# Spaced weight pieces, a later second block and split evictions in a fused attention, feed-forward and top-1 expert kernel

## The chip, the cores and the metric

One core of a Trainium2 chip runs the whole kernel. The metric is the device time of one launch in microseconds (us); lower is better. The profile comes from one execution of the same program.

## The reference, cut to what matters

Three layers follow each other: causal attention with a forget gate, a dense feed-forward layer, and a mixture of eight experts of which each token uses one. The change touches the middle layer alone.

```python
def _moe_ref(x, w_in, w_out):            # x: 2304 x 512, w_in: 512 x 2048, w_out: 2048 x 512
    h = x @ w_in
    g = np.where(h >= 1, h, np.where(h <= -1, 0.0, (h + 1) ** 2 / 4))
    return (g @ w_out).astype(np.float32)

x = attention(q, k, v, f)                # 4 x 8 heads x 576 tokens x 64, brought to 2304 x 512
x = _moe_ref(x, w_in, w_out)             # the weights are float64
return _moe2_ref(x, ...)                 # gate, 8 experts of 512 x 1024 x 512, top 1
```

## The kernel before, in words

**Precision.** Each product is made of three matmuls: operands are split into a high and a low part (`h`, `l`), and high x high, low x high and high x low are summed. So an activation block needs a cast and a subtraction (ACT and DVE for a loaded block, ACT and POOL for hidden values), and so does a weight.

**Halves.** The hidden width of 2048 is done in two halves of 1024, each with its own layer object: `half0` (tiles `hp`, `accp`, weights `wa`) starts while attention still runs; `half1` (tiles `hr`, `accr`, `accBr`, weights `wb`) follows and adds the stored result of half0. Then comes the expert layer (`hm`, `accm`). A half works through token blocks. Half0 has five blocks of 256 tokens and then two of 512 (n = 5 and 6); half1 has four of 512 and one of 256. A block has eight units, one for each 128 hidden columns: a first product (`first`, 12 matmuls into one hidden bank `hp` or `hr`), a middle on the vector engines (`ffn_hidden`: ACT `tp`, DVE `gp` twice, ACT `ghp`, POOL `glp`), and a second product (`ffn_second`, 12 matmuls into four accumulators of one PSUM bank each for a wide block). There are two hidden banks, two pairs of `gh`, `gl`, one `t`, one `g`, and one set of accumulators.

**Weights.** `float64_weights` loads a half's weights in 16 pieces of 512 KB (a0, b0, a1, b1, ... a7, b7: `a` serves a unit's first product, `b` its second). A piece is a DMA on SP's queue (L819) and a serial chain on one working buffer `wx`: ACT L828, DVE L829, L831, L833, L835, ACT L839, POOL L840. Two raw buffers (`wr_b`) and one working buffer (`wx_b`) are all there is.

**The order.** All instructions are put in order by a planner when the program is built: generators ask for engines and buffers, and the planner takes its own prices and its own clock (`o.now`, in ns) to decide which operation is next on which engine. On the chip only the order of each engine's queue and the waits on data are left: a time in the planner holds nothing back on the chip, it only places an operation behind others. Every queue, SP's too, runs in order. The planner's price for a wide unit's two products is

```python
def mm(n, k=1):
    return k * max(111.0, n * 0.458)      # 2 x mm(512, 12) = 5628 ns
```

**Around the change.** `late_pools` runs when attention's last result is stored; it makes half1's weights object and starts its 16 pieces with the due times `[0.0] * 2 * NF`, so that a piece starts as soon as a raw buffer is free. When half0's last first product is planned (`half0.first_done`), `half1.loads` asks for its blocks 0 and 1, for which there are buffers; `load_wide` issues four DMAs for a block and then four pairs of ACT L870 and DVE L871. `ffn_finish0` empties the accumulators of a wide block of half0, one after another: ACT L1051 (`x_0a`), DVE L1048 (`x_0b`), ACT (`x_1a`), DVE (`x_1b`). The next block's second products wait for this.

Of the kernel before, what the change touches and what calls it, by code (L numbers as in the profile page):

```python
# [14 lines left out]
ALU = mybir.AluOpType  # L15
# [3 lines left out]
P = 128  # L19
# [5 lines left out]
def f32(ap):  # L25
    return ap.bitcast(F32)
# [12 lines left out]
NP_ = 8  # L39
NSUM = 4  # L40
FIRST_WEIGHTS = [6000.0 + 2700.0 * n for n in range(5)] + [20500.0 + 5200.0 * n for n in range(11)]
WARM_FROM, WARM = 1500.0, 0.6


# [31 lines left out]
class Order:  # L76
# [90 lines left out]
    def done(self, ev):  # L167
        ev.n -= 1
        if ev.n == 0:
            for g in ev.waiters:  # L170
                self.at(self.now, lambda g=g: self.step(g, None))
            ev.waiters = []

    def give(self, res, ids):
        res.ids += ids
        while res.waiters:
            gen, n = res.waiters[0]
            got = res.take(n)
            if got is None:
                return  # L180
            res.waiters.pop(0)
            self.at(self.now, lambda gen=gen, got=got: self.step(gen, got))
# [8 lines left out]
def dve(n, fn, prio=5.0, fast=False):  # L191
    return Use("DVE", 144 + n * (0.6 if fast else 1.05), fn, prio)


def act(n, fn, prio=5.0, more=0.0):
    return Use("ACT", 155 + n / 1.2 + more, fn, prio)
# [10 lines left out]
def dma(nbytes, fn, prio=5.0, eng="SP", k=1):  # L207

    hold = 550.0 if eng == "SP" else 1000.0

    def after(o):
        o.dma_free = max(o.dma_free, o.now + hold + 650.0) + nbytes / 245.0
        return max(o.dma_free, o.now + hold * k + 650.0 + nbytes / k / 245.0) + 1000.0
    return Use(eng, hold * k, fn, prio, after)
# [9 lines left out]
def kernel(  # L224
# [14 lines left out]
    nc = tc.nc  # L239
# [6 lines left out]
    KC = DM // P  # L246
    TB = 256
# [3 lines left out]
    FH = w_in.shape[1] // 2  # L251
    NF = FH // P
# [11 lines left out]
    o = Order()  # L264
    go, give, done = o.spawn, o.give, o.done
# [509 lines left out]
    def wide_x(ids, name):  # L775

        gp = late["gp"]
        if ids[0] == 2:
            t = gp.tile([P, 2, KC, 2 * TB], F32R, tag="xA", name=name, bufs=1)
            return [[t[:, hl, c] for c in range(KC)] for hl in range(2)]  # L780
        t = gp.tile([P, 2, 2, 2 * TB], F32R, tag="xB", name=name, bufs=1)
        f = [fp.tile([P, 2, 2 * TB], F32R, tag=f"x{n}0", name=name + n, bufs=1) for n in "hl"]
        return [[f[hl][:, 0], f[hl][:, 1], t[:, hl, 0], t[:, hl, 1]] for hl in range(2)]
# [16 lines left out]
    def float64_weights(W, src_a, src_b, times, prio):  # L800

        a = src_a.rearrange("(c p) f -> p c f", p=P)
        b = src_b.rearrange("(c p) d -> p c d", p=P)
        ah, al, bh, bl = W.t
        n = 0
        for fc in range(NF):
            cs = slice(P * fc, P * fc + P)
            for src, hi, lo, ok in ((a[:, :, cs], ah[:, :, cs], al[:, :, cs], W.ok[0][fc]),
                                    (b[:, fc:fc + 1], bh[:, fc:fc + 1], bl[:, fc:fc + 1],
                                     W.ok[1][fc])):  # L810
                yield times[n]
                g = yield (wr_b, 1)
                go(float64_piece(g, src, hi, lo, ok, W.name, prio))
                n += 1
# [44 lines left out]
    def load_wide(src, w, ok, name, ev):  # L859
        yield ok  # L860
        g = yield (xl_b, ((2,), (0, 1)))

        def put():
            hi, lo = wide_x(g, name)
            for c in range(KC):
                nc.sync.dma_start(f32(lo[c])[:, :w], src[c])
            return hi, lo
        hi, lo = yield dma(P * KC * w * 4, put, 1, k=4)
        for c in range(KC):
            yield act(w, lambda: nc.scalar.copy(hi[c][:, :w], f32(lo[c])[:, :w]), 1)  # L870
            yield dve(w, lambda: nc.vector.tensor_tensor(  # L871
                lo[c][:, :w], f32(lo[c])[:, :w], f32(hi[c])[:, :w], ALU.subtract), 1)
        ev.x = ([x[:, :w] for x in hi], [x[:, :w] for x in lo], g)
        done(ev)
# [46 lines left out]
    class Layer:  # L921
# [15 lines left out]
        def loads(self):  # L937
            for n in self.blocks:
                if self is half0 and n < NARROW:
                    if n == 0:  # L940
                        continue
                    yield self.src_ok[n]
                    go(load_block(self.src[n], self.src_ok[n], f"{self.name}x{n}", self.x_ok[n]))
                else:
                    yield self.src_ok[n]
                    go(load_wide(self.src[n], self.widths[n], self.src_ok[n], f"{self.name}x{n}",
                                 self.x_ok[n]))

# [59 lines left out]
    def ffn_second(acc, fc, W, gh, gl):  # L1008
        bh, bl = W.t[2:]
        narrow = acc[0].shape[1] == TB  # L1010
        w = gh.shape[1]
        for ip, (b, g) in enumerate(((bh, gh), (bl, gh), (bh, gl))):
            for d in range(KC):
                nc.tensor.matmul(acc[d][:, :w], b[:, fc, P * d:P * d + P], g,  # L1014
                                 start=(fc == 0 and ip == 0 and (not narrow or d % 2 == 0)),
                                 stop=(fc == NF - 1 and ip == 2), skip_group_check=True)

    def moe_second(acc, fc, W, gh, gl):
        bh, bl = W.t[2:]
# [13 lines left out]
    def keep(dst, r, ok, g):  # L1033
        def put():
            for i in range(2):
                nc.sync.dma_start(dst[2 * i:2 * i + 2].rearrange("c p t -> p c t"), r[i])
        yield dma(P * KC * TB * 4, put, 2, k=2)
        done(ok)
        if g is not None:
            give(x2_b, g)  # L1040

    def ffn_finish0(n, acc):
        if n >= NARROW:
            g = yield (x2_b, ((0, 1),))
            r = wide_r(f"x2_0_{n}")
            for d in range(KC):
                if d % 2:
                    yield dve(2 * TB, lambda: nc.vector.tensor_scalar(r[d], acc[d], 4.0, None,  # L1048
                                                                      ALU.mult), 0)
                else:  # L1050
                    yield act(2 * TB, lambda: nc.scalar.mul(r[d], acc[d], 4.0), 0)  # L1051
            go(keep_first(n, r, g))
            return
        g = yield (x2_b, 1)
        r = [x.rearrange("p (d t) -> p d t", d=2) for x in x2_half(g[0], f"x2_0_{n}")]
        acc = late["acc0"]
        yield act(2 * TB, lambda: nc.scalar.mul(r[0], acc[:, 0:2], 4.0), 0)
        yield dve(2 * TB, lambda: nc.vector.tensor_scalar(r[1], acc[:, 2:4], 4.0, None,
                                                          ALU.mult), 0)
        go(keep(x2p[n], r, x2p_ok[n], g))  # L1060

    def keep_first(n, r, g):
        t0, w = FIRST[n]
# [53 lines left out]
    def late_pools():  # L1117

        yield att_ok
        psa.release()  # L1120
        ap.release()
        late["wp2"] = tc.alloc_tile_pool(name="wp2", bufs=1, side="right")
        late["gp"] = gp = ctx.enter_context(tc.tile_pool(name="gp", bufs=1))
        late["psg"] = ctx.enter_context(tc.tile_pool(name="psg", bufs=1, space=PSUM))
        late["nat_b"] = Buffers(2)
        late["gt_b"], late["gl_b"] = Buffers(1), Buffers(1)
        give(h_b, [1])
        give(xl_b, [1, 2])
        give(x2_b, [1])
        W = late["W1"] = Weights(late["wp2"], "wb")  # L1130
        go(float64_weights(W, w_in[:, FH:], w_out[FH:], [0.0] * 2 * NF, 4))
        for n, shape, dt in (
            ("es", [E, 2], F32),
            ("ie", [P, KC, P + E], F32), ("itau", [P, 1], F32), ("iota", [P, E], F32),
            ("tid", [P, NTT], I32), ("ones", [P, P], F32), ("upper", [P, P], F32),
            ("sidx", [P, NSLOT], F32), ("tinit", [P, NROW // P, 2], F32), ("ss", [P, 2, NTT], F32),
            ("lg", [P, NTT, E], F32), ("oh", [P, NTT, E], F32), ("gate", [P, NTT], F32),
            ("gj", [P, DM], F32), ("fold", [P, Q], F32), ("gm", [P, NTT - TL], F32),
        ):
            G[n] = gp.tile(shape, dt, name=n)  # L1140
        go(gate_setup())
        go(prev_loads())
        done(late_ok)
# [476 lines left out]
    def static_slots():  # L1620
# [11 lines left out]
        for ok in late_w["M"].ok[0] + late_w["M"].ok[1]:  # L1632
# [8 lines left out]
    half1 = Layer("r", wide, lambda: late["W1"], xw, [att_ok] * NW, ffn_hidden, ffn_second,  # L1641
                  ffn_finish1, 6)
# [23 lines left out]
    with tc.manual_schedule():  # L1666
        go(attention())
        go(float64_weights(W0, w_in[:, :FH], w_out[:FH], FIRST_WEIGHTS, 0.8))
        go(phases())
# [40 lines left out]
```

## Time and profile before

| | us |
|---|---|
| median of three runs | 875.53 (872.15 to 875.68) |
| the profiled execution, its device time | 871.14 |
| its span from the first to the last instruction | 869.5 |
| TensorE (PE) busy | 844.2 |
| DVE, ACT, POOL busy | 466.9, 362.4, 309.8 |

The profiled execution's own time is its span and 1.6 us around it. A busy PE counts matmuls that overlap: a matmul of 512 columns is listed with some 0.39 us, while the next starts 0.23 us after it.

### The profile page before, as it was taken

The page shows a single profiled execution, that of the slowest core. Times are in us where ns is not written, and L with a number is a line of the kernel's source. Part 1 is how long each engine was busy: PE and PEld are TensorE (multiplying, and loading weights), DVE is VectorE, ACT ScalarE, POOL GpSimd, SP SyncE. Part 2 cuts the span into 40 slices and gives each one's busy share as a digit, 9 for nine tenths or more (in the row PEclk, how much of TensorE's full clock was granted, in tenths as well). Part 3 has the DMA queues.
Part 4 walks back from the last instruction along what each step waited for, and adds up shares of the span by engine and source line. Part 5 has one row for each costly group of instructions (what it writes and reads, how often), then busy time and mean ns, then how long its engine had stood idle before and what let it go on. Part 6 is the DMA issues. An engine that isn't in the chain of part 4 may idle for free.

```text
span 869.5 us, 14316 instructions
## 1 busy us (share of the span) xinstructions
PE 844.2 (97%) x5000; PEld 674.6 (78%) x5000; DVE 466.9 (54%) x1112; ACT 362.4 (42%) x845; POOL 309.8 (36%) x407
## 2 busy tenths in 40 slices
PE   9998998999999999998899999999999999999996
PEld 7766876877787798876688888888898888887585
DVE  7798977656645537777752545367552531212121
ACT  5677666556556635333532333323342121212110
POOL 3566866555545534444532112321210033100000
PEclk9999999999999999999899999999999999999999
DMA  7999666574324154223521133555432111541220
GB/s 141 179 189 198 165 151 145 120 143 118 104 76 133 37 181 78 72 73 122 171 95 49 72 123 103 176 170 176 149 132 89 49 49 49 196 167 49 97 74 25
DMA packets 152264, 101.91 MB, mean 117 GB/s; under 512 B 102866, under 2 KB 121810, under 8 KB 152192
## 3 DMA queue, kind: packets, MB, share of 16 engines
q1 hardware_dynamic: 149024, 96.22, 40.2%
q0 software_dynamic: 2832, 4.22, 1.8%
q8 instruction: 40, 0.66, 0.3%
q10 hardware_dynamic: 336, 0.56, 0.2%
q14 instruction: 32, 0.26, 0.1%
HBM read 76.86 MB, written 24.49 MB: 117 GB/s over the span
## 4 chain that ended last, share of the span: by engine, by line
PE 84%; DVE 6%; POOL 3%; issue 2%; ACT 2%; DMA 1%; SPq 0%; POOLq 0%; DVEq 0%; ACTq 0%
PE hr L885 12%; PE hm L885 12%; PE accp L1014 7%; PE hp L885 7%; PE accr L1014 6%; PE accBr L1014 6%; PE accm L1026 6%; PE accBm L1026 6%; PE SR L537 5%; PE X L657 4%; PE T L617 4%; PE warm L734 2%; POOL wb L840 2%; PE SR L532 1%; PE gt L1222 1%
## 5 line engine op out<-in xcount | busy, mean ns | idle before, releaser
L907 POOL TENSOR_TENSOR glr<-gr,ghr 128x512 fp32r<-128x512 f32 x36 | 47.1, 1308 | 151.6 <-PE accBr L1014 74.3
L885 PE MATMUL hr<-rx,wb 128*128 128x512 f32 (+1 forms) x384 | 90.1, 369 | 0.0
L603 POOL TENSOR_SCALAR P<-P,st 128x512 f32<-128x512 f32 (+3 forms) x128 | 76.3, 609 | 37.9 <-DVE st L599 23.8
L885 PE MATMUL hm<-mx,wm 128*128 128x512 f32 (+1 forms) x336 | 87.0, 379 | 0.0
L592 ACT ACTIVATE P<-P,st 128x512 f32<-128x512 f32 (+3 forms) x128 | 71.4, 558 | 31.1 <-DVE st L587 30.4
L916 DVE SCALAR_TENSOR_TENSOR glm<-hm,ghm 128x512 fp32r<-128x512 f32 x36 | 24.8, 690 | 103.0 <-PE accBm L1026 68.4
L915 ACT ACTIVATE ghm<-hm 128x512 fp32r<-128x512 f32 x36 | 21.5, 598 | 132.4 <-PE accBm L1026 120.5
L885 PEld LDWEIGHTS hr<-rx,wb 128*128 128x128 f32 x384 | 66.2, 189 | 13.3
L885 PEld LDWEIGHTS hm<-mx,wm 128*128 128x128 f32 x336 | 61.0, 188 | 14.9 <-issue 3.4
L907 POOL TENSOR_TENSOR glp<-gp,ghp 128x512 fp32r<-128x512 f32 x36 | 53.4, 1483 | 53.7 <-ACT ghp L906 44.2
L1014 PE MATMUL accp<-ghp,wa 128*128 128x256 f32 (+1 forms) x384 | 67.7, 309 | 2.2 <-ACT ghp L906 2.1
L1014 PEld LDWEIGHTS accp<-ghp,wa 128*128 128x128 f32 x384 | 52.6, 190 | 8.3 <-ACT ghp L906 3.0
L587 DVE CUSTOM_DVE_ANT_0 P<-SR,cm 128x512 f32<-128x512 f32 (+3 forms) x96 | 45.2, 485 | 25.0 <-PE SR L537 23.2
L617 PE MATMUL T<-ident,P 128*128 128x128 f32 x320 | 52.5, 279 | 2.6 <-POOL P L603 2.1
L901 DVE SCALAR_TENSOR_TENSOR gr<-tr 128x512 f32<-128x512 f32 x36 | 25.9, 718 | 48.0 <-POOL glr L907 27.6
L637 ACT COPY pt<-T 128x512 f32<-128x512 f32 (+2 forms) x96 | 35.3, 391 | 37.5 <-PE T L617 36.7
L537 PE MATMUL SR<-kt,qt 64*128 64x384 f32 (+3 forms) x224 | 45.7, 485 | 4.2 <-DVE st L587 4.1
L897 ACT ACTIVATE tr<-hr,quarter 128x512 f32<-128x512 f32 x36 | 24.7, 687 | 58.9 <-PE hr L885 29.1
L617 PEld LDWEIGHTS T<-ident,P 128*128 128x128 f32 x320 | 36.9, 141 | 14.0 <-POOL P L603 4.5
L1014 PE MATMUL accr<-ghr,wb 128*128 128x512 f32 (+1 forms) x160 | 47.0, 375 | 0.0
L1014 PE MATMUL accBr<-ghr,wb 128*128 128x512 f32 (+1 forms) x160 | 46.5, 372 | 0.0
L1026 PE MATMUL accm<-wm,ghm 128*128 128x512 f32 x144 | 46.2, 394 | 0.0
(345 smaller groups left out, 1886.9 us busy)
## 6 DMA issues: line engine op xcount, KB each, us to landing
cm<-rows SPq DMA_DIRECT2D x24, 256.0 KB, 4.4
rawq<-in_q_dram SPq DMA_DIRECT2D x64, 72.0 KB, 3.8
rawk<-in_k_dram SPq DMA_DIRECT2D x64, 72.0 KB, 3.0
xs<-xT SPq DMA_DIRECT2D x16, 288.0 KB, 2.2
x2n<-nat SPq DMA_DIRECT2D x18, 256.0 KB, 3.3
war<-in_moe_w_in_dram SPq DMA_DIRECT2D x8, 512.0 KB, 4.4
war<-in_moe_w_out_dram SPq DMA_DIRECT2D x8, 512.0 KB, 4.9
rawv<-in_v_dram SPq DMA_DIRECT2D x32, 128.0 KB, 2.7
```

The source lines that it names most:

```text
L537: nc.tensor.matmul(bank[:, j, :w], qt[p, P * c:P * c + P], kt[p, :w], start=True, stop=i >= NSUM)
L587: yield dve(w + 80, lambda: nc.vector.tensor_tensor_reduce(out=pv_, in0=so, in1=m, scale=-0.125, scalar=3e38, op0=ALU.add, op1=ALU.min, ac ...
L592: yield act(w, lambda: nc.scalar.activation(pw, pw, AF.Exp, bias=st[:, n:n + 1], scale=-1.0, accum_out=st[:, 2 + n:3 + n]), 1, 330)
L603: yield pool1(w, lambda: nc.gpsimd.tensor_scalar(pw, pw, st[:, 6 + n:7 + n], 1.0, ALU.mult, ALU.mult), 0)
L617: nc.tensor.transpose(T[:, P * n:P * n + P], p[:, P * kb:P * kb + P], ident)
L637: yield act(n, lambda: nc.scalar.copy(dh, src), 0)
L657: nc.tensor.matmul(X[D * j:D * j + D, P * kb:], vt[:, kb, j], pt[i, j][0][:, 512 * kb:512 * kb + 512 - P * kb], start=(kb == 0), stop=(kb ...
L885: nc.tensor.matmul(oo, a[:, c, cs], x[c], start=(ip == 0 and c == 0), stop=(ip == 2 and c == KC - 1))
L901: yield dve(n, lambda: nc.vector.scalar_tensor_tensor(g, t, 0.5, t, ALU.min, ALU.mult), 2)
L907: yield pool2(n, lambda: nc.gpsimd.tensor_tensor(gl, g, f32(gh), ALU.subtract), 1)
L1014: nc.tensor.matmul(acc[d][:, :w], b[:, fc, P * d:P * d + P], g, start=(fc == 0 and ip == 0 and (not narrow or d % 2 == 0)), stop=(fc == NF ...
L1026: nc.tensor.matmul(acc[a * (4 // na)], g[:, P * a:P * a + P], b[:, fc], start=(fc == 0 and ip == 0), stop=(fc == NF - 1 and ip == 2))
```

## The change

Four edits. (1) Piece n of half1's weights is not started before the planner's time at `late_pools` plus 8500 ns times n. (2) Half1's block 1 is loaded only after half1's first hidden unit is planned to be done. (3) In the last unit of a block the 12 second products are ordered by accumulator (three for the first, then three for the second, and so on) rather than by part; this holds for both halves and for narrow blocks. (4) In half0's wide blocks the accumulators are emptied by two generators that don't wait for each other: ACT takes 0 and 2, DVE takes 1 and 3.

```diff
+PACE = 8500.0
...
                     yield self.src_ok[n]
+                    if self is half1 and n == 1:
+                        yield self.g_ok[0, (0,)]
                     go(load_wide(self.src[n], self.widths[n], self.src_ok[n], f"{self.name}x{n}",
                                  self.x_ok[n]))
...
-        for ip, (b, g) in enumerate(((bh, gh), (bl, gh), (bh, gl))):
-            for d in range(KC):
-                nc.tensor.matmul(acc[d][:, :w], b[:, fc, P * d:P * d + P], g,
-                                 start=(fc == 0 and ip == 0 and (not narrow or d % 2 == 0)),
-                                 stop=(fc == NF - 1 and ip == 2), skip_group_check=True)
+        todo = [(ip, d) for ip in range(3) for d in range(KC)]
+        if fc == NF - 1:
+            todo.sort(key=lambda t: t[1])
+        for ip, d in todo:
+            b, g = ((bh, gh), (bl, gh), (bh, gl))[ip]
+            nc.tensor.matmul(acc[d][:, :w], b[:, fc, P * d:P * d + P], g,
+                             start=(fc == 0 and ip == 0 and (not narrow or d % 2 == 0)),
+                             stop=(fc == NF - 1 and ip == 2), skip_group_check=True)
...
-            for d in range(KC):
-                if d % 2:
-                    yield dve(2 * TB, lambda: nc.vector.tensor_scalar(r[d], acc[d], 4.0, None,
-                                                                      ALU.mult), 0)
-                else:
-                    yield act(2 * TB, lambda: nc.scalar.mul(r[d], acc[d], 4.0), 0)
+            out_of = Event(2)
+            go(first_out(r, acc, 0, out_of))
+            go(first_out(r, acc, 1, out_of))
+            yield out_of
...
+    def first_out(r, acc, odd, ev):
+        for d in range(odd, KC, 2):
+            if odd:
+                yield dve(2 * TB, lambda: nc.vector.tensor_scalar(r[d], acc[d], 4.0, None,
+                                                                  ALU.mult), 0)
+            else:
+                yield act(2 * TB, lambda: nc.scalar.mul(r[d], acc[d], 4.0), 0)
+        done(ev)
...
-        go(float64_weights(W, w_in[:, FH:], w_out[FH:], [0.0] * 2 * NF, 4))
+        go(float64_weights(W, w_in[:, FH:], w_out[FH:],
+                           [o.now + PACE * n for n in range(2 * NF)], 4))
```

## Rows read from the trace of the kernel before

**Rows 1.** The page: the span, and busy time by engine.

```profile
span 869.5 us, 14316 instructions
PE 844.2 (97%) x5000; PEld 674.6 (78%) x5000; DVE 466.9 (54%) x1112; ACT 362.4 (42%) x845; POOL 309.8 (36%) x407
```

**Rows 2.** Windows: stretch and length; busy time (instructions) by engine, granted clock, DMA share, GB/s.

```profile
442.00:470.00 28.00, 28.00 (x122) 22.55 (x121) 10.62 (x15) 7.65 (x13) 9.43 (x7) 1.00 0.00 1
656.00:790.00 134.00, 134.00 (x595) 109.80 (x593) 39.24 (x101) 26.90 (x50) 19.71 (x20) 1.00 0.27 95
...
344.80:366.93 22.13, 22.13 (x98) 18.02 (x96) 15.95 (x22) 9.53 (x16) 11.81 (x8) 1.00 0.27 80
366.93:383.43 16.50, 16.50 (x74) 13.51 (x72) 11.34 (x15) 6.15 (x10) 7.97 (x6) 1.00 0.27 85
383.43:398.76 15.33, 13.19 (x50) 9.93 (x49) 11.53 (x16) 5.83 (x10) 6.06 (x4) 0.89 0.41 137
398.76:412.41 13.65, 11.53 (x49) 8.85 (x48) 9.62 (x14) 4.85 (x9) 6.66 (x4) 1.00 0.24 77
412.41:432.81 20.40, 16.12 (x62) 11.99 (x61) 14.54 (x22) 10.25 (x19) 12.84 (x6) 0.86 0.55 181
```

**Rows 3.** Waits of PE from 310 to 440 us: total, times, longest.

```profile
PE hp L885 <- ACT tp L897: 2.4, 3, 1.4
...
PE accp L1014 <- ACT ghp L906: 2.1, 1, 2.1
```

**Rows 4.** Timeline of PE: start, length, line, tile, count, wait before it.

```profile
392.00 0.73 PE L1014 MATMUL accBp<-ghp,wa 128*128 128x512 f32 x2 [1.82 <-DVE x_1b L1048]
...
393.93 1.05 PE L1014 MATMUL accp<-glp,wa 128*128 128x512 f32 x2
...
430.93 1.22 PE L1014 MATMUL accp<-glp,wa 128*128 128x512 f32 x2 [2.10 <-POOL glp L907]
...
432.81 9.07 PE L885 MATMUL hr<-rx,wb 128*128 128x512 f32 x36
...
466.88 2.96 PE L885 MATMUL hr<-rx,wb 128*128 128x512 f32 x12
```

**Rows 5.** The chain of waits from 383 to 433 us, in order of time.

```profile
401.73 0.67 ACT wbx L828
...
403.35 0.70 DVE wbx L833
404.08 1.67 DVE wbx L835
...
406.47 1.76 POOL wb L840
408.25 0.67 ACT wbx L828
```

**Rows 6.** Timelines of ACT and of DVE where half0's block 5 is emptied.

```profile
387.00 0.66 ACT L828 ACTIVATE wbx<-wbr 128x512 f32<-128x512 f32 x1 [0.36 <-POOL wb L840]
387.56 0.58 ACT L1051 ACTIVATE x_0a<-accp 128x512 f32<-128x512 f32 x1
...
391.26 0.68 DVE L1048 TENSOR_SCALAR x_1b<-accBp 128x512 f32<-128x512 f32 x1
```

**Rows 7.** Timeline of all engines from 412 to 452 us, where half0 ends.

```profile
412.71 2.66 SPq L866 DMA_DIRECT2D rx<-xs  x4
...
421.21 1.29 POOL L907 TENSOR_TENSOR glp<-gp,ghp 128x512 fp32r<-128x512 f32 x1
...
426.04 4.84 POOL L907 TENSOR_TENSOR glp<-gp,ghp 128x512 fp32r<-128x512 f32 x1 [3.53 <-issue]
...
430.36 1.07 DVE L871 TENSOR_TENSOR rx<-rx 128x512 fp32r<-128x512 f32 x1 [0.60 <-ACT rx L870]
```

**Rows 8.** SP's queue, the first piece's issue; and the issues of half1's `a` pieces (KB, us to landing).

```profile
318.07 0.55 SPq L819 DMA_DIRECT2D wbr<-in_moe_w_in_dram  x1
...
wbr<-in_moe_w_in_dram SPq DMA_DIRECT2D x8, 512.0 KB, 4.1
```

## The prediction, made before the change was run

> **What bounds the kernel now.** I read the page first: PE is busy for 97% of the span [rows 1], so the kernel is bound by PE, and the question is where PE waits or runs at a lower clock. The table of windows shows it. From 442 us on PE has no gap: both rows of that part show it busy all through at clock 1.00 [rows 2]. So what the edits do to half1's and the experts' blocks can't take anything off there. The loss lies in half0's two wide blocks.
>
> Its size follows from counting. In 344.80:366.93 PE does four units (96 matmuls; the rows count one or two more that began before the edge), 5.53 us each; in 366.93:383.43 three units, 5.50 each [rows 2]. That is 0.23 us a matmul and the pace with no loss. The next three stretches hold 48, 48 and 60 matmuls (2, 2 and 2.5 units), so 11.04, 11.04 and 13.80 us; they took 15.33, 13.65 and 20.40 [rows 2]. Lost: 4.3, 2.6 and 6.6, together 13.5 us. The 36 matmuls that open half1 at 432.81 are listed with 9.07 us [rows 4] where 36 x 0.233 is 8.4; some 0.5 of that is still lower clock. So 14.0 us is all that this change can win.
>
> **Why it is lost.** The chain of waits says it: from 383 to 433 it runs through the weight pieces, not through PE. One turn, from L828 at 401.73 to the next L828 at 408.25, is 6.52 us [rows 5]. The pieces are started back to back, each waits for the working buffer that the one before frees with its POOL operation, and the planner has laid one unit beside each. On the chip every queue runs in order, so a unit's `tp` stands behind an L828 that waits for POOL, and PE's units take 6.52 us instead of 5.5. In block 5 PE lived on a lead of three first products; by 386 us the lead is used up, and PE waits for `tp` three times (2.4 us) [rows 3]. At the turn from block 5 to block 6 the same L828 holds ACT until 387.00, and `x_0a` starts at 387.56, 4.1 us after the block's last product was issued (383.43, the window's edge); `x_1b` follows at 391.26 [rows 6], and PE has waited 1.82 us for it by 392.00 [rows 4]. After such a gap the pairs of matmuls take 1.05 us [rows 4] and the granted clock of the stretch falls to 0.89 (0.86 at the end of half0) [rows 2], so each gap costs nearly its own length again.
>
> **Edit 1, the pieces.** Nothing is removed: 16 DMAs and 112 vector instructions stay. What moves is their place in the queues. 8.5 us of planner time is 1.51 units of 5.628 us, so one piece now stands beside a unit and a half, which PE needs 1.51 x 5.5 = 8.3 us for; the piece's own turn remains 6.5 and no L828 meets a busy working buffer. The 2.6 us of the middle stretch should nearly vanish: 2.3 taken, between 1.3 (half of it) and 2.6. SP's queue gets easier too: a piece's DMA there waits for a raw buffer and holds up all behind it, such as `rx` at 412.71 [rows 7]; spaced, the buffer has long been free.
>
> Two inputs in SBUF make DVE and POOL get in each other's way: L833 takes 0.70 us and L835 beside a POOL operation 1.67, `wb` on POOL 1.76 [rows 5] against 1.29 for a POOL operation of that shape alone [rows 7]. Take this as one door that only one may use. A turn of 6.52 us passes four such DVE operations (0.70) and two of POOL (1.29) through it, 5.4 us or 83%. Spaced, 1.51 units and a piece pass 5 and 2.5, 6.7 us; at the same 83% they need 8.1 us, and PE 8.3. So the door is just wide enough, and this is a rival below. The Trainium skill has it as a rule (SBUF — State Buffer, section Who interferes with whom): a DVE instruction with two SBUF inputs and a GpSimd instruction that reads SBUF exclude each other for the whole instruction; by that rule, the 1.67 is waiting and not slower work, the trace agrees, and spacing frees none of it, because no such instruction is removed.
>
> **Edits 3 and 4, the turn of the block.** Now two engines empty two accumulators each without waiting for each other: some 0.58 on ACT and 0.68 on DVE apiece [rows 6], so 1.4 us and a gap, where 8.5 us lay between 383.43 and the end of `x_1b`. PE still has two first products to do there (5.5 us), so even with one piece operation of 1.67 between the two on DVE the accumulators are free in time. Of 4.3 I take 3.8; at least 2, if ACT or DVE reach the evictions as late as half of now. The order by accumulator alone is worth nothing: it lets the first eviction start 9 x 0.23 = 2.1 us earlier, but ACT comes to it 4 us late now, and in half1, where DVE empties everything in a row, PE has no gap to give [rows 2]. Three matmuls in a row into one bank cost no more: a first product puts 12 in a row, at the same pace.
>
> **Edit 2 and the handover to half1.** Of 6.6 us, 2.1 is a wait for `ghp` [rows 3], 2.1 for a `glp` that POOL takes 4.84 us for, beside DVE's run of splits for blocks 0 and 1, against 1.29 alone [rows 7], and the rest is lower clock and small gaps. Half of the splits (four on ACT, four on DVE, 0.68 each) and four of eight DMAs go behind half1's first unit. There they are hidden: block 1 is needed after eight units, 45 us, and load and split took 18.7 now (412.71 to 431.43) [rows 7]. Block 0 remains: four DMAs and four splits, at best some 12 us, against the four or five second products (2.76 each, 11 to 14 us) that PE still has after its last first product. That nearly covers it. I take 4.6 of 6.6; at least 1, if block 0 now arrives last; at most all.
>
> The slow start of half1 goes with the gap before it: 0.3 of 0.5 (0 to 0.5).
>
> **What the pieces cost later.** Pieces 12 to 15 now lie beside half1's first units. Before, the last ones did too, after 432 us, and PE lost nothing from 442 on [rows 2]; I take 0. If each cost what a piece costs in 398.76:412.41 (2.6 for two), it is 5.2. And they must be there in time: from the first DMA at 318.07, piece 14 (a7) starts at 318 + 14 x 8.5 = 437, lands 4.1 us later [rows 8] and takes one turn of 6.5: 448. It is needed 34.1 us after half1's start (466.88 - 432.81) [rows 4]; with half1 starting at 421.6 that is 456. Margin 8 us.
>
> **The sum.** 3.8 + 2.3 + 4.6 + 0.3 = 11.0 us, all before half1; what follows only moves. From the bounds: 2 + 1.3 + 1 + 0 = 4.3 to 14.0. The profiled execution would come to 871.1 - 11.0 = 860.1. It lies 4.4 us under the median of the runs shown, so I put the predicted time against that median: 875.5 - 11.0 = 864.5 us.
>
> **The rivals.**
> - *The handover stays the bound* (the door between DVE and POOL, or block 0's load): half0's units run at PE's pace, but the last `glp` or the last split of block 0 comes late, and what was won in the middle is waited for at the end. For it: the door has 2% to spare, and block 0's four splits add 2.8 us to it; 12 us of load against 11 to 14 of cover. Only 1 or 2 of the 6.6 is won and the middle is halved: 4 to 8 us in all, 867.5 to 871.5. The Trainium skill's rule named above is the one that speaks for it.
> - *Nothing is won, the loss moves*: the four pieces beside half1's first units cost 1.3 each, 5.2, and the handover keeps its 6.6; 11.0 - 4.6 - 5.2 leaves about 1. Against it: half1's stretch now shows vector engines with room (DVE 10.62 of 28) [rows 2]. 872 to 877.
> - *Slower: a7 is late.* If a piece needed 8 us more than one landing and one turn, PE would stand still for each us beyond that, and at lower clock after. To end above 880 it would have to be about 8 + 11 + 4.4 = 23 us late (half that, if clock doubles it). The page's pieces show nothing near this.
>
> **Chances.** Forecast (861 to 867) 0.60; handover 0.22; moved 0.11; slower 0.07. What this kernel's measurement can tell from no change is 0.5%, 4.4 us, so under 871.1 is faster: 0.60 and nearly all of 0.22, 0.80; same 0.13; slower 0.07. The range leaves out the last two cases in part: 859.5 (16 us won, a little over the bound, for the spread of the runs) to 872.
>
> **What would show it.** Right: from about 345 us to half1's start at about 421.6 units keep 5.5 us, no wait for `x_1b`, clock 1.00, the pieces' L828 8 us apart and no longer waiting for POOL; half1 without gaps. Wrong: a wait for `rx`, `glp` or `wb` between 415 and 460, or gaps after half1's start. The step most likely to fail is the 4.6 of the handover.

## The result, and the profile after

The changed kernel takes 861.23 us (median of 6 runs, 859.77 to 863.84), the kernel before 874.41 (6 runs, 869.99 to 875.68). The ratio is 0.9861 [0.9833, 0.989]: 12.2 us faster, 9.6 to 14.6. The forecast was 864.5, in a range of 859.5 to 872, from a sum of 11.0 us.

The page of the changed kernel, span and busy time:

```profile
span 861.3 us, 14317 instructions
PE 840.4 (98%) x5000; PEld 672.7 (78%) x5000; DVE 463.9 (54%) x1112; ACT 361.9 (42%) x845; POOL 306.4 (36%) x407
```

As many matmuls and vector instructions as before [rows 1], and a span that is 8.2 us shorter. That is less than 12.2, and the trace says why. From the first matmul of half0's block 5 to half1's fourth first product the kernel before needs 114.30 us (330.37 to 444.67), the changed one 102.37 (331.79 to 434.16): 11.9 less. From there to the last DMA issue at the end both need 418.93 (444.67 to 863.60, 434.16 to 853.09). But this execution came to block 5 1.4 us later, and ran on for 7.8 us after that last issue had ended, where the one before ran on for 5.5. Over the fourteen kernels traced here block 5 begins between 329.54 and 334.42 us and the tail is 5.5 to 7.9 us, in no order of the edits, so I don't count either for the change; -11.9 + 1.4 + 2.3 is the 8.2. So below, beside the times, each kernel is given by this stretch: **the changed stretch**, 114.30 us before. With nothing lost in it, it would be 114.30 - 14.0, some 100.3.

Windows of the changed kernel, cut at the same places of the work as [rows 2] (the last unit of block 5; block 6's first products; its last second products; half1's opening; then eight units):

```profile
384.85:391.05 6.20, 5.80 (x25) 4.42 (x24) 4.10 (x8) 3.89 (x7) 2.54 (x2) 1.00 0.52 179
391.05:410.33 19.28, 19.28 (x86) 15.76 (x84) 11.45 (x17) 7.24 (x13) 8.80 (x7) 1.00 0.43 139
410.33:422.04 11.71, 11.19 (x50) 8.93 (x48) 9.08 (x11) 5.19 (x10) 4.88 (x4) 1.00 0.11 37
422.04:431.00 8.96, 8.74 (x37) 6.41 (x36) 6.32 (x10) 3.43 (x7) 1.29 (x1) 1.00 0.70 239
431.00:475.00 44.00, 44.00 (x190) 35.47 (x189) 30.41 (x42) 18.92 (x32) 18.65 (x13) 1.00 0.26 89
```

The matmuls between block 5's last turn and half1 are the same 156 as before, laid out a little differently: 24, 84 and 48 here. At 5.5 us for 24 they would take 5.5, 19.25 and 11.0; they take 6.20, 19.28 and 11.71. Lost: 0.7, nothing, 0.7, where it was 4.3, 2.6 and 6.6. The granted clock is 1.00 in every row, where it was 0.89, 1.00 and 0.86. The last row shows that nothing moved into half1: eight units in 44.00 us, 5.5 each, with PE busy all through, although three pieces still lie there. Half1's opening did not get better: its 36 first matmuls take 8.96 us here, where 36 x 0.233 is 8.4.

Half of the 2.1 us that are left over the 100.3 is named by the waits of PE in the changed kernel, 300 to 450 us, all rows:

```profile
PE accp L1020 <- POOL glp L908: 0.5, 1, 0.5
PE accBp L1020 <- ACT x_1a L1072: 0.4, 1, 0.4
PE hr L886 <- DVE rx L872: 0.2, 1, 0.2
```

The waits of [rows 3] for `tp` and `ghp`, and the one of [rows 4] for `x_1b`, are gone. The wait for `glp`, 2.1 us in [rows 4], is down to 0.5. The chain of waits in the changed kernel, from 360 to 425 us:

```profile
367.67 0.68 ACT wbx L829
...
372.42 1.75 POOL wb L841
374.20 0.67 ACT wbx L829
...
396.71 2.78 PE hp L886 x12
...
402.21 2.78 PE hp L886 x12
```

(The lines of the kernel have moved on by one: L828 is L829 here, L840 is L841.) Up to 386 us it still runs through the pieces, and their turn is still 374.20 - 367.67 = 6.53 us, as in [rows 5]. From 391 to 412 us it is PE's own matmuls, a unit each 5.50 us; from there to half1's first matmuls it runs through ACT and DVE, at last through block 0's splits. In ACT's queue the reason can be counted: before, from 387.00 to 408.25, the order was piece, `tp`, piece, piece, `tp`, piece; in the changed kernel from 374.20 on, two units and one unit stand in turn between one piece and the next, 1.5 on the mean, as 8.5 us of planner time should give. Ahead of that, in most of block 5, the changed kernel's pieces stand one to a unit and run at the times of before (the POOL operations of four of them begin at 345.24, 359.30, 372.42 and 378.95; before at 345.14, 358.97, 372.01 and 378.70). PE has its lead there, so it costs nothing.

The turn of block 5, as ACT and then DVE show it in the changed kernel:

```profile
386.04 0.60 ACT L1072 ACTIVATE x_0a<-accp 128x512 f32<-128x512 f32 x1
386.68 0.69 DVE L1069 TENSOR_SCALAR x_0b<-accp 128x512 f32<-128x512 f32 x1 [1.24 <-ACT x_0a L1072]
387.29 0.68 DVE L1069 TENSOR_SCALAR x_1b<-accBp 128x512 f32<-128x512 f32 x1
388.00 0.60 ACT L1072 ACTIVATE x_1a<-accBp 128x512 f32<-128x512 f32 x1 [0.85 <-DVE x_1b L1069]
```

The four evictions take 2.6 us from first to last (386.04 to 388.60), 4.4 in [rows 6] (387.56 to 391.94). But they still go one after another: `x_0b` waits for `x_0a`, though the two read different accumulators, and `x_1a` for `x_1b`. Edit 4 gave them generators of their own; the wait between them on the chip is still there. And PE has less to do meanwhile: the kernel before put two first products of block 6 ahead of its first second product (24 matmuls, from 383.43), the changed kernel puts one (12, from 384.85). So the evictions have 2.8 us to hide behind and not 5.5.

### The profile page after: what moved, and what is told of

It reads as the page before. It is cut to its first block, busy times and chain, and to the rows that moved or that the text cites. A ratio compares the mean times of both kernels' runs of the same rounds, so it can differ in the third digit from the quotient of the medians.

```text
span 861.3 us, 14317 instructions
## 1 busy us (share of the span) xinstructions
PE 840.4 (98%) x5000; PEld 672.7 (78%) x5000; DVE 463.9 (54%) x1112; ACT 361.9 (42%) x845; POOL 306.4 (36%) x407
## 4 chain that ended last, share of the span: by engine, by line
PE 83%; DVE 7%; POOL 2%; issue 2%; DMA 2%; ACT 2%; SPq 0%; ACTq 0%; DVEq 0%; POOLq 0%
PE hm L886 12%; PE hr L886 12%; PE hp L886 9%; PE accp L1020 6%; PE accr L1020 6%; PE accBr L1020 6%; PE accm L1032 6%; PE accBm L1032 6%; PE SR L538 4%; PE T L618 4%; PE X L658 4%; PE gt L1236 1%; PE U L711 1%; PE SR L533 1%; PE T_None L618 1%
## 5 line engine op out<-in xcount | busy, mean ns | idle before, releaser
L908 POOL TENSOR_TENSOR glp<-gp,ghp 128x512 fp32r<-128x512 f32 x36 | 49.8, 1383 | 55.1 <-ACT ghp L907 48.2
L1032 PE MATMUL accBm<-wm,ghm 128*128 128x512 f32 x144 | 45.8, 392 | 0.0
```

What stands on the lines that cost most here:

```text
L908: yield pool2(n, lambda: nc.gpsimd.tensor_tensor(gl, g, f32(gh), ALU.subtract), 1)
L1032: nc.tensor.matmul(acc[a * (4 // na)], g[:, P * a:P * a + P], b[:, fc], start=(fc == 0 and ip == 0), stop=(fc == NF - 1 and ip == 2))
```

## The experiments

Theory A: the gain is edit 1's. A piece is a chain of 6.5 us on in-order queues; laid one to a unit, it makes the unit as long as itself, and spacing takes the pieces off PE's path at the turn, in the middle and at the handover alike. The rival (Theory B in the expectations) is the sum as predicted: edits 3 and 4 bring the turn's 3.8, edit 2 the handover's 4.6, and edit 1 only 2.3. All results, the difference worked out from the ratio and the median of before beside it (873.45, 873.92 and 873.62 in the three sets), the changed stretch from one execution each:

| kernel | edits | median us | ratio | us to before | changed stretch |
|---|---|---|---|---|---|
| changed | 1 2 3 4 | 861.23 | 0.9861 [0.9833, 0.989] | -12.2 | 102.37 |
| e1 | 1 | 862.30 | 0.9873 [0.9854, 0.9892] | -11.1 | 102.31 |
| e2 | 2 3 4 | 871.40 | 0.9977 [0.9965, 0.9989] | -2.0 | 112.72 |
| e3 | 1 3 4 | 863.04 | 0.9876 [0.9856, 0.9896] | -10.8 | 104.66 |
| e4 | 1 2 | 859.32 | 0.9831 [0.9811, 0.985] | -14.8 | 100.72 |
| e5 | 1 2 3 | 860.42 | 0.985 [0.9831, 0.9869] | -13.1 | 101.66 |
| e6 | none; `lo` on DVE | 862.44 | 0.9861 [0.9845, 0.9878] | -12.1 | 102.13 |
| e7 | all, 5500 ns | 868.94 | 0.9947 [0.9929, 0.9965] | -4.6 | 110.68 |
| e8 | all, 10000 ns | 860.96 | 0.9844 [0.9826, 0.9862] | -13.6 | 101.69 |
| e9 | 2 | 869.29 | 0.994 [0.9918, 0.9961] | -5.2 | 110.21 |
| e10 | 4 | 872.09 | 0.9982 [0.997, 0.9993] | -1.6 | 113.07 |
| e11 | all, 14000 ns | 882.99 | 1.0108 [1.0091, 1.0125] | +9.4 | 101.14, loses later |
| e12 | 1 2; `lo` on DVE | 860.07 | 0.985 [0.9834, 0.9867] | -13.1 | 100.67 |

### Which edit it is

**e1, the spacing alone**: the kernel before with edit 1.

```diff
-        go(float64_weights(W, w_in[:, FH:], w_out[FH:], [0.0] * 2 * NF, 4))
+        go(float64_weights(W, w_in[:, FH:], w_out[FH:],
+                           [o.now + PACE * n for n in range(2 * NF)], 4))
```

> Edit 1 alone (the pieces spaced by 8.5 us of planner time; block 1 loaded as before, evictions as before). Theory A, that the chained weight pieces are what holds half0's units and the turn of its blocks: 8 to 11 us faster than the kernel before, and PE's waits for tp between 345 and 412 us gone; the wait for x_1b shrinks from 1.8 to under 0.8 us, because ACT no longer stands on a piece there. Theory B, that the two visible waits (evictions at the turn, splits of two blocks at the end) make the loss: 2 to 4 us faster, with both waits still there.

**e2, all but the spacing**: the changed kernel without that edit.

```diff
-        go(float64_weights(W, w_in[:, FH:], w_out[FH:],
-                           [o.now + PACE * n for n in range(2 * NF)], 4))
+        go(float64_weights(W, w_in[:, FH:], w_out[FH:], [0.0] * 2 * NF, 4))
```

> The changed kernel without edit 1: block 1 late, order by accumulator and split evictions stay, the 16 pieces are chained again. Theory A: at most 3 us faster than before, a piece's turn 6.5 us from 359 to 412 us, PE waiting for tp. Theory B: 8 us faster or more.

e1 gains 11.1 us, e2 2.0. So edit 1 alone has all but the whole gain (a little over the 8 to 11 expected), and edits 2, 3 and 4 together, without it, some two. PE's waits between 300 and 450 us, first in e1 (all rows), then in e2 (the three longest):

```profile
PE accBr L1016 <- DVE x_1b L1050: 0.5, 1, 0.5
PE hr L886 <- DVE rx L872: 0.5, 1, 0.5
```

```profile
PE accp L1020 <- DVE x_0b L1069: 2.5, 1, 2.5
PE accp L1020 <- ACT ghp L907: 1.9, 1, 1.9
PE hr L886 <- ACT rx L871: 1.4, 1, 1.4
```

In e2 the wait at the turn, 1.82 for `x_1b` in [rows 4], is now 2.5 for `x_0b`. The evictions end 6.4 us after the block's last product was issued (382.74 to 389.16), where it was 8.5. But `x_0a` still starts 4.1 us after that product (386.86), behind an L829 that POOL's `wb` lets go, and PE has only one first product to do meanwhile, as in the changed kernel. The wait for `tp` that was expected in e2 isn't there. The chain of waits in e2 runs through the pieces as before, with the same turn (415.09 - 408.56 = 6.53):

```profile
408.56 0.67 ACT wbx L829
...
413.30 1.76 POOL wb L841
...
415.09 0.67 ACT wbx L829
```

**e9, the later block alone, and e10, the evictions alone.** Each is the kernel before with one edit, so that what they do without spacing is seen singly.

```diff
+                    if self is half1 and n == 1:
+                        yield self.g_ok[0, (0,)]
```

> Edit 2 alone on the kernel before. The pieces are still chained, so block 6's units stay at 6.5 us and PE's waits for tp stay; only the handover from half0 to half1 gets lighter: 0 to 4 us faster, at most the prediction's term for the handover (4.6 us).

```diff
...
+            go(first_out(r, acc, 0, out_of))
+            go(first_out(r, acc, 1, out_of))
+            yield out_of
...
```

> Edit 4 alone on the kernel before (the order of the products as before). The wait for x_1b of 1.8 us at the turn may shrink, but ACT still comes to it late behind a piece: 0 to 3 us faster. The prediction's term for the turn (3.8 us), if it belonged to this edit: 3 to 4 us faster.

e9 gains 5.2 us (3.4 to 7.2), 4.1 in the changed stretch: more than the 0 to 4 expected, and about the 4.6 that the prediction gave edit 2. e10 gains 1.6. With both and edit 3, e2 gains only 2.0. So the edits don't add up, with the pieces still in the way. PE's waits from 300 to 480 us in e10 show what its edit does by itself, two rows:

```profile
PE hr L886 <- ACT rx L871: 5.0, 2, 4.2
PE accp L1016 <- DVE x_0b L1065: 2.6, 1, 2.6
```

The wait for `tp` in block 6 is gone, and a wait of 4.2 us for `rx` at half1's start has come in its place. The windows of e10 tell what was won and where it was given back (the turn, 24 matmuls; the middle, 84; half0's last 48; half1's opening, 48):

```profile
384.23:394.59 10.36, 7.53 (x25) 5.37 (x24) 7.27 (x12) 4.79 (x9) 4.25 (x3) 0.85 0.45 160
394.59:414.01 19.42, 19.42 (x85) 15.88 (x84) 14.53 (x19) 7.46 (x13) 8.42 (x7) 0.99 0.25 78
414.01:425.12 11.11, 11.11 (x49) 8.93 (x48) 7.14 (x11) 5.09 (x9) 6.18 (x4) 1.00 0.81 283
425.12:444.25 19.13, 14.10 (x50) 10.65 (x49) 15.20 (x24) 10.39 (x18) 5.84 (x5) 0.82 0.40 137
```

Without any spacing the middle loses 0.2 us and half0's last products 0.1; the turn loses 4.9 and the opening 8.1. The middle of e2 lost nothing either (84 matmuls in 19.28 us, from 391.63). So a piece of 6.5 us beside a unit does not always hold the unit; why it doesn't in this order was not followed up. What it costs then lies at the opening: four DMAs bring `rx`, and SP issues them at 414.13 in e10 and at 413.05 in e2, right behind a piece's DMA that waited for its raw buffer.

### What the other edits are worth once the pieces are spaced

**e3, the changed kernel without edit 2; e4, without edits 3 and 4; e5, without edit 4 alone.**

```diff
-                    if self is half1 and n == 1:
-                        yield self.g_ok[0, (0,)]
```

> The changed kernel without edit 2: half1's block 1 is loaded together with block 0. Theory A: the handover from half0 to half1 has room once the pieces are spaced, so 0 to 2 us slower than the changed kernel. Theory B and the prediction's own term for the handover (4.6 us): 3 to 5 us slower than the changed kernel, with PE waiting for glp or for block 0's split between 410 and 430 us.

```diff
-        if fc == NF - 1:
-            todo.sort(key=lambda t: t[1])
...
-            go(first_out(r, acc, 0, out_of))
-            go(first_out(r, acc, 1, out_of))
-            yield out_of
+            for d in range(KC):
+                if d % 2:
+                    yield dve(...)
+                else:
+                    yield act(...)
```

> The changed kernel without edits 3 and 4: products of the last unit by part, evictions one after another. Theory A: the turn needs neither, 0 to 1 us slower than the changed kernel. The prediction's term for the turn, if it belongs to these edits: 3 to 4 us slower, with a wait for x_1b of 1.5 us or more.

(e5 has the second part of this diff and keeps the sort.)

> The changed kernel without edit 4, with edit 3: the last products by accumulator, but the evictions one after another again. If the loss against the kernel without edits 3 and 4 comes from the two eviction generators (DVE is planned to empty accumulator 1 before the last split of block 0 of half1, and waits there for the last products): as fast as the kernel without both, about 859.5 us, and half1 starts with no gap of PE. If it comes from the order of the products: as the changed kernel, about 861.5 us.

e3: the changed stretch is 2.3 us longer without edit 2, and by the ratios the kernel 1.3 slower, with overlapping intervals; e1 against e4, the same edit taken out, says 1.6 and 3.7, with intervals that don't overlap. So edit 2 is worth some 1.3 to 3.7 us beside edit 1. In e3 PE waits for half1's first `tr`, one row of its waits from 300 to 480 us:

```profile
PE hr L886 <- ACT tr L898: 2.1, 1, 2.1
```

that is, for an ACT operation which block 1's loading has been put in front of. e4, with edits 1 and 2 alone, has the lowest median of all, 859.32, though its interval overlaps that of the changed kernel. In its trace half1 starts without a gap; a window of its first 11.2 us:

```profile
421.00:432.20 11.20, 11.20 (x50) 9.02 (x49) 6.90 (x13) 5.33 (x9) 3.84 (x3) 1.00 0.80 266
```

From half1's first matmul to its fourth first product e4 needs 11.34 us and the changed kernel 12.12, and the timeline of DVE and PE in the changed kernel shows where a part of the 0.8 goes:

```profile
422.04 1.80 PE L886 MATMUL hr<-rx,wb 128*128 128x512 f32 x7
...
422.68 0.68 DVE L1069 TENSOR_SCALAR x_0b<-accp 128x512 f32<-128x512 f32 x1
423.28 0.68 DVE L872 TENSOR_TENSOR rx<-rx 128x512 fp32r<-128x512 f32 x1
...
424.52 0.69 DVE L1069 TENSOR_SCALAR x_1b<-accBp 128x512 f32<-128x512 f32 x1 [0.56 <-ACT x_1a L1072]
```

DVE empties accumulator 1 first and only then makes the last split of block 0; the eighth matmul of half1 waits for that split. The planner, with evictions free to go as soon as an engine is, put one in front of a split that PE needs sooner. e5, which has edit 3 but not the generators, has no such gap at half1's start either. Nor has PE a wait for an eviction at the turn in e1, e4 or e5, which empty the accumulators in the old way and keep two first products there; 0.4 us of wait for `x_1a` is left in the changed kernel. e5 and e4 differ by 1.1 us in the median and 0.9 in the changed stretch, with overlapping intervals; PE waits 0.6 us for `glp` in e5, which the order by accumulator needs at the third product of half0's last unit and not at the ninth, and not at all for it in e4. Edits 3 and 4 were each worth nothing that a time here can tell, and the traces speak against both rather than for them.

### Is it the spacing, or the length of the turn?

**e6, the piece's last subtraction on DVE, no spacing.** The kernel before, with POOL's part of the chain (1.76 us at the chip) moved, so that the piece gets shorter while one piece still stands beside each unit.

```diff
-        yield pool2(DM, lambda: nc.gpsimd.tensor_tensor(lo, xv, f32(hi), ALU.subtract), prio)
+        if name == "wb":
+            yield dve(DM, lambda: nc.vector.tensor_tensor(lo, xv, f32(hi), ALU.subtract), prio)
+        else:
+            yield pool2(DM, lambda: nc.gpsimd.tensor_tensor(lo, xv, f32(hi), ALU.subtract), prio)
```

> The kernel before, with one thing changed: the last step of a piece of half1's weights (the subtraction that gives the low part) is done by DVE in place of POOL. No spacing, no other edit; a piece still stands beside each unit of half0's second wide block. A piece's turn should fall from 6.5 to some 5 us. Theory A, that the turn of 6.5 us beside a unit of 5.5 us is what holds PE: 7 to 11 us faster than before, units of block 6 at 5.5 us. Rival, that it is the amount of piece work beside a unit and only spacing helps: 0 to 3 us faster, or slower, since DVE has more to do.

It gains 12.1 us, as much as the four edits together. ACT's timeline in e6:

```profile
375.39 0.67 ACT L829 ACTIVATE wbx<-wbr 128x512 f32<-128x512 f32 x1 [0.76 <-DVE wb L842]
...
380.83 0.68 ACT L829 ACTIVATE wbx<-wbr 128x512 f32<-128x512 f32 x1 [0.76 <-DVE wb L842]
```

The turn is 380.83 - 375.39 = 5.44 us now, just under a unit. The chain of waits of e6 from 364 to 400 us is PE's own, and windows beside it:

```profile
371.29 2.78 PE hp L889 x12
...
376.79 2.78 PE hp L889 x12
```

```profile
370.00:386.00 16.00, 16.00 (x71) 13.11 (x70) 15.01 (x21) 7.39 (x12) 4.63 (x3) 1.00 0.28 93
386.00:402.00 16.00, 16.00 (x71) 13.09 (x71) 13.46 (x23) 8.39 (x14) 2.88 (x3) 1.00 0.54 169
402.00:415.00 13.00, 13.00 (x59) 10.66 (x58) 9.23 (x16) 5.52 (x9) 4.29 (x3) 1.00 0.67 230
```

The first window lies in block 5, where the kernel before lost nothing either. The other two hold the turn and block 6, where it lost 6.9 us: here PE has no gap, with still a piece to each unit and DVE busy for 13.46 of 16.00 us. So, in the order of the kernel before, neither the number of pieces beside a unit nor DVE's load was the cost, but that the chain was longer than the unit. e6 takes work from POOL besides; that this isn't the cause is seen in the changed kernel, whose middle stretch loses nothing with POOL busy for 46% of it (8.80 of 19.28 us), against 49% before (6.66 of 13.65 us) [rows 2].

**e12, both**: e4's edits 1 and 2, and e6's subtraction on DVE.

> Spacing of 8.5 us and block 1 late, evictions and products as before, and the last step of a piece on DVE as in the run that shortened the turn. If spacing and the shorter turn cure the same thing, nothing adds up: 858 to 861 us, as with spacing and late block 1 alone. If they were two things: 850 us or less.

860.07 us and a changed stretch of 100.67, e4's 100.72 again and about the 100.3 of a stretch without loss. PE has no wait listed at all from 300 to 480 us. The two remedies cure the same thing; their gains don't add.

### How far apart the pieces may be

**e7, e8 and e11, other spacings** in the changed kernel: less than the turn, a little more than now, and far more.

```diff
-PACE = 8500.0
+PACE = 5500.0        # e7; 10000.0 in e8, 14000.0 in e11
```

> The changed kernel with a spacing of 5.5 us in place of 8.5, which is less than a piece's turn and about one unit. Theory A: pieces and units are coupled nearly one to one again and most of the gain is lost, 867 to 871 us. If any due time does it (for instance because the first pieces start later): 860 to 863 us.

> The changed kernel with a spacing of 10 us in place of 8.5. Piece 14 (a7) comes 14 x 1.5 = 21 us later than at 8.5, where it was there about 4 us before its unit. The prediction's slower rival: PE waits 10 to 17 us in half1's first block, 871 to 878 us, with the wait on POOL's last step of a piece. If the weights' margin is larger than worked out: 860 to 863 us.

> The changed kernel with a spacing of 14 us, where PE surely needs weights that come late in the order. If a due time acts on the chip only by the place in the queues: the pieces left when half1 starts (about nine) run at their turn of 6.5 us, 55 us against the 45 us of block 0, so 5 to 20 us slower than the changed kernel, 866 to 881 us. If a due time were a time on the chip: piece 14 would come 77 us later than at 8.5 us, and the kernel would take over 915 us.

e7, below the turn of 6.5, gives back 7.6 of the 12.2 us. Its waits are those of e2 and e10, which have no spacing, two of its rows:

```profile
PE hr L886 <- ACT rx L871: 3.0, 2, 2.0
PE accp L1020 <- DVE x_0b L1069: 1.4, 1, 1.4
```

As in those, the middle loses nothing (84 matmuls in 19.28 us, from 392.18): the loss is 4.1 us at the turn, 1.1 in half0's last products and 5.6 at half1's opening, and SP issues `rx` at 411.40.

e8 was expected to starve half1 of a7 and lose; by its time it lost nothing (-13.6 us). The expectation, as the prediction's margin, took a due time for a time on the chip. It isn't: the first piece was issued at 317.39, so that piece 14 would be due at 317.39 + 14 x 10 = 457.4, but SP issued it 14 us earlier. SP's queue, then POOL's and PE's timeline of e8:

```profile
443.02 0.38 SPq L820 DMA_DIRECT2D wbr<-in_moe_w_in_dram  x1
...
459.29 1.89 PE L886 MATMUL hr<-rx,wb 128*128 128x512 f32 x7
...
459.31 1.29 POOL L841 TENSOR_TENSOR wb<-wbx,wb 128x512 fp32r<-128x512 f32 x1 [1.28 <-ACT wb L840]
```

POOL finishes a7's low part at 460.6, after PE has begun the unit, but the first eight matmuls of a first product use the high part only, so it is in time by some 0.6 us. The planner had helped: it laid three units' second products in a row ahead of a7's first product, which begins 40.3 us after half1's start (459.29 - 419.01), against 34.3 in the changed kernel. From half1's fourth first product to the last DMA issue e8 needs 0.7 us more than the changed kernel.

e11 is slower than before, by 9.4 us, and so 21.8 over the changed kernel, a little more than the 5 to 20 expected and far from the time that due times on the chip would give. Its waits of PE between 300 and 480 us, the first row; a window; and the chain:

```profile
PE accr L1020 <- ACT wb L840: 14.2, 2, 7.1
```

```profile
460.00:480.00 20.00, 8.96 (x26) 6.57 (x27) 9.41 (x14) 4.56 (x8) 5.63 (x5) 0.71 0.19 57
```

```profile
453.72 3.08 PE hr L886 x12
456.82 0.70 ACT tr L898
...
459.51 0.66 ACT wbx L829
...
463.23 0.63 ACT wb L840
...
468.99 3.08 PE hr L886 x12
```

One unit now takes 468.99 - 453.72 = 15.27 us, and the granted clock is 0.71. The queues couple the other way round: a late piece stands on ACT behind `tr` of the unit before it, so a unit waits for its piece, and the next piece for that unit.

## Why the prediction was right, point by point

**What bounds, and the bound.** Right. The loss was 14.0 us between block 5 and half1's opening; the best versions (e4, e12) bring the stretch to 100.7, within half a us of the floor, and gain 13 to 15 by the ratio. Nothing was won or lost from half1's fourth first product on (418.93 us in both).

**The terms, by place.** The turn: 3.8 predicted, 4.3 - 0.7 = 3.6 measured. The middle: 2.3 and 2.6. The handover: 4.6 and 5.9; this, named as likeliest to fail, was too small by 1.3. The opening: 0.3 and -0.3; measured on the 48 matmuls from half1's start to the end of the changed stretch, it took 12.12 us against 11.86. Together, by the changed stretch, 11.9 against 11.0. (By the prediction's own terms half1 would start at 432.8 - 10.7 = 422.1, not at its 421.6, since the 0.3 lies behind the start; it started at 422.04.) The base was 1.1 high (875.53 of three runs, 874.41 of six), so the time came out 3.3 under the forecast, by 0.9 of the sum, 1.1 of the base, and the rest in the spread of runs between medians and ratio.

**What failed: who brings the terms.** The prediction gave the turn's 3.8 to edits 3 and 4, on the ground that two engines would now "empty two accumulators each without waiting for each other", and the handover's 4.6 to edit 2. e1 has neither and gains 11.1. All three places lost time to one cause, which the prediction had named under "Why it is lost": pieces that stand ahead of PE's work in in-order queues. It saw ACT's; at the turn it is DVE's too (before, `x_1b` comes behind L833 and L835, from 389.10 on), and at the handover SP's, where `rx` stands behind a piece's DMA. Once the pieces are spaced, the evictions and the splits are on time in the old form too. Where they are not spaced, edit 4 removes one wait and meets another (e2, e10). The premise that PE still has two first products at the turn held in the old form alone; with edit 4 it has one. Edit 3 was put at nothing; no time here tells it from nothing (e4 against e5), though it wasn't run alone. That the sum came out although its owners were wrong is luck in part: the four edits were measured together, and the losses by place, which the windows gave, were nearly all won back by one of them.

**Edit 2** is worth something by itself (5.2 us in e9), and 1.3 to 3.7 beside edit 1. But that block 0's `rx` comes early is edit 1's doing: SP issues it at 402.18 in the changed kernel, at 391.88 in e1 and at 400.27 in e3, where it was 412.71 [rows 7] and is 413.06 in e9, with edit 2 and no spacing. In all five a piece's DMA ends on SP's queue just before it. That is what the paragraph on edit 1 said of SP's queue, and put no number on.

**Signs that were wrong.** "The pieces' L828 8 us apart and no longer waiting for POOL": from 346 to 381 us they stand 6.5 to 7.1 us apart, as before, and four of those six wait 1.8 to 2.1 us for POOL. The spacing shows in the order from 374 us on, just where PE's lead was used up. The chain of waits of before, which runs through the pieces already in block 5, didn't tell where PE pays for it; the windows did. Nor does "each gap costs nearly its own length again" hold for every gap: in [rows 2] the stretch with two waits for `tp` is at clock 1.00, and so is e2's turn (382.74:391.63) with its wait of 2.5 us; it held at the turn (0.89) and the handover (0.86) of the kernel before.

**The rivals.** The door between DVE and POOL (0.22) did not decide. In the middle stretch PE lost nothing with DVE at 11.45 and POOL at 8.80 of 19.28 us, and e6 puts more on DVE without harm. The rule of the Trainium skill (SBUF — State Buffer, section Who interferes with whom) that spoke for it isn't contradicted: a subtraction that reads two SBUF tiles still takes POOL 1.75 us here in place of 1.29. What spacing changed is that little on PE's path waits behind it. That the loss moves into half1 (0.11) is what e10 did, by `rx` and not by the late pieces, and not what the whole change did. The slower rival, a7 late (0.07), has a margin of 4 us rather than 8: a7's second part is ready at 452.4 and its unit begins at 456.37. a7 was issued 6 us before the 437 of the prediction (431.01), but its L829 came only at 443.55, after the piece before it had freed the working buffer (439.7) and behind other work on ACT. To come true the rival needs a spacing over 10 us: e8 was in time by 0.6 us, e11 shows all of it, and nothing between the two was run.

**What stays open.** Whether edits 3 and 4 cost the 0.9 and 0.7 us that the traces of e4, e5 and the changed kernel show (1.6 together) is not settled by the times, whose intervals overlap. Why the middle of e2, e7 and e10 loses nothing without a useful spacing is open too. Why the planner still lays one piece to a unit in most of block 5, with 8.5 us between due times, was not followed up.

## What to carry to other kernels

When a serial chain runs beside a loop on in-order queues, compare its turn with the loop's period: with 6.5 us against 5.5 the kernel before lost 2.6 us in two units as soon as the lead was gone, and shortening the turn below the period (e6) or laying the chain out at more than its turn (e1) each won it back; doing both won nothing more. The cost need not show in the loop: in e2, e7 and e10 it came out at the block's turn and at the next load, which stands behind the chain's DMA in its queue. Spacings of 8.5 and 10 us did alike, the second just in time; 5.5, below the turn, lost most of the gain, and 14 starved the consumer. When several waits show at different places of one stretch, ask for one cause first: pricing each edit by the wait nearest to it gave the right sum and the wrong owners.

## What was not expected of the hardware

Two evictions from different accumulators of one tile, on ACT and on DVE, were expected to overlap; one waits for the other to end, 1.24 and 0.85 us at block 5's turn and 0.90 at block 6's. Evictions from the two tiles do overlap: in e2 `x_0b` runs from 387.47 to 388.16 on DVE, `x_1a` from 387.84 on ACT. Whether the chip asks for the wait or the program's own dependence on the tile was not tried. And the time from the end of the last DMA issue to the end of the span is not fixed: 5.5 us in the profiled execution before, 7.8 in the one after.
